# Loading and transposing the second batch's q and k in another split and order, in a fused attention and gate kernel

## The chip, the core and the metric

The kernel runs on one core of a Trainium2 chip. The metric is the device time of one execution in microseconds; the time shown for a kernel is the median of several executions.

## What is computed

Attention over 4 batches, 8 heads, 768 positions and a head size of 64, in which a query sees the 128 positions that end with its own and the first 4 positions of the sequence (sinks), and behind it a highway layer on the 3072 rows of 512:

```
scores = q @ k.T / 8, kept where 0 <= query - key < 128 or key < 4
a = softmax(scores);  x = a @ v            # heads side by side: 3072 x 512
H = relu(x @ w_h);  T = sigmoid(x @ w_t + b_t)
out = T * H + (1 - T) * x                  # float32
```

All inputs are float32 in the chip's main memory. Matrix products run in float16 with float32 sums.

## The kernel before

**Steps.** The 3072 rows are cut into 24 tiles n of 128 rows, 6 for each batch. The program is written as one loop over n, in which the stages of several tiles are interleaved, and the order in which the calls stand is the order on each engine: a last pass chains the instructions of every engine in that order, so that no engine overtakes itself. In step n stand the scores of tile n, the values of tile n-1 and the gate of tile n-2.

- `opening(n, n-1, n-2)` puts the mask matmuls (L308, L318), the 32 score matmuls of tile n (L333, `product`), the bias of the gate (L371) and the sink part (L379) on TensorE. In steps 5 and 6 the scores stand alone (`scores(n)`), then `hidden` of an older tile, and then the rest of the opening. The scores of tile c of a batch take the q of tiles c and c+1 (two column blocks) and the k of tile c.
- `expo(n)`: ScalarE's exponential E (L421), 128x2048, in the last tile of a batch 128x1024. Its starts mark the steps in the text: E(n).
- `values(n-1)`: TensorE, E times v (L432, L435), needs the v tile in float16, made by `cast_v` (L150), on VectorE up to tile 5 and on GpSimd (POOL) from tile 6 on.
- `norm(n-1)`: VectorE, reciprocal (L443) and product X (L445). Then `x_transpose` (L461) on TensorE and `x_copy` (L466) on ScalarE.
- `gate(n-2)` (L471) with w_t, `tanh` (L479), `hidden` (L492) with w_h into the one buffer `ps_h`, `diff` (L505, VectorE, reads `ps_h`), later `gated` (L510), `finish` (L516, mostly POOL) and the store. Since w_h is loaded late, `hidden(0)` and `diff(0)` stand in step 4, `hidden(1)`, `diff(1)` and `hidden(2)`, `diff(2)` in step 5, `hidden(3)` in step 6.

**Loads.** q and k are cast to float16 on the way by DMAs that POOL issues; POOL's queue also carries w_t, w_h and the bias. A batch's positions are split in `segments`: three thirds of 256 for batches 0 and 1, two halves of 384 for batches 2 and 3; they are called (batch, part) here, as in q(1,0). `load_part` (L117) loads one of the four row groups g of a part: 32 partitions, 2 head groups, 64 KB as float16 in a third. Four of them make a part of q or k. v comes by `load_v` (L140) from SyncE, 256 KB a tile; the loads of v(2) to v(7) are tied to the score matmuls of an earlier step.

Before the loop POOL issues k(0,0), k(0,1), w_t, the bias, q(0,2), k(0,2) and w_h; then, in step 2, the sink values of batch 0, q(1,0) and k(1,0), and from there a written list of counts for each step:

```
issues = [(b, i, g, which) for b in range(1, B) ...][2 * G:]
for n, count in zip(range(2, 17), [4] * 4 + [3] * 7 + [2] + [3] * 3):
    loads[n] = [issues.pop(0) for _ in range(count)]
```

so that q(1,1), k(1,1), q(1,2), k(1,2) stand in steps 2 to 5, and batch 2 begins in step 6. From step 6 on POOL's turn in a step is `cast_v`, loads, `finish` of older tiles (`completed`).

**Transposes.** `transpose_qk` (L133) transposes 32x32 blocks of a loaded part on VectorE, from `nat` to `tr`: 128x512 float32 words for a whole third, both head groups at once. `units` says in which step: q(1,0) in step 4, k(1,0) in step 5, ahead of `diff(1)` and `norm(4)`, q(1,1) in 6, k(1,1) and q(1,2) in 7, k(1,2) in 8. Of batch 0, q(0,2) is transposed in step 2 and k(0,2) in step 3, both behind the step's `norm`.

Of the kernel before, what the change touches and what calls it, by code (L numbers as in the profile page):

```python
# [37 lines left out]
def kernel(  # L38
# [14 lines left out]
    pe, act, dve, pool, sp = nc.tensor, nc.scalar, nc.vector, nc.gpsimd, nc.sync  # L53

    B, H, S, D = q.shape
# [10 lines left out]
    G = 4  # L66
# [43 lines left out]
    def v_of(n):  # L110
        return vt[n % 8]

    def load_part(b, i, g, which, into=None, engine=pool):

        t0, nt = segments[b][i]
        into = nat[b][i][:, which] if into is None else into
        engine.dma_start(  # L117
            out=into[32 * g:32 * g + 32].rearrange("p hg m d -> p hg (m d)"),
            in_=(q, k)[which][b, :, t0:t0 + nt, :].rearrange(
                "(hg g) (r m) d -> g r hg (m d)", g=G, m=nt // 32)[g])  # L120

    def load_rows(b, i, which):
        for g in range(G):
            load_part(b, i, g, which)

    def transpose_qk(b, i, which, hgs=slice(0, HG)):

# [9 lines left out]
    def load_v(n, after=None):  # L137
        b, t = divmod(n, NC)
        V32[n] = work.tile([P, H, D], FP32, tag="V32", name="V32", bufs=8)
        ins = sp.dma_start(out=V32[n],  # L140
                           in_=v[b, :, t * P:(t + 1) * P, :].transpose([1, 0, 2]))
        if after is not None:
            tc.add_manual_dep(
                ins.ins, after.ins.name,
                mybir.DependencyInfo(
                    mybir.DependencyClass.Sync, mybir.DependencyReason.DATA),
                reason="behind the loads needed first")

    def cast_v(n, engine):
        engine.tensor_copy(out=v_of(n)[:, :, 0:D], in_=V32[n])  # L150
# [32 lines left out]
    def load_sinks(b, gs=range(G)):  # L183
        for g in gs:
# [7 lines left out]
    load_rows(0, 0, 1)  # L192
# [7 lines left out]
    load_v(1)  # L200
    load_sinks(0, range(2, G))
    make_identity(nc, ident)
    load_rows(0, 1, 1)
    pool.dma_start(out=wt, in_=moe_w_t.rearrange("(kc p) of -> p kc of", p=P))
    pool.dma_start(out=brow[0:P:32, :], in_=moe_b_t.unsqueeze(0).to_broadcast([G, DM]))
    load_rows(0, 2, 0)
    load_rows(0, 2, 1)
    pool.dma_start(out=wh, in_=moe_w_h.rearrange("(kc p) of -> p kc of", p=P))

    dve.memset(ebias, _EXP_BIAS)  # L210
# [337 lines left out]
    for b in range(1, B):  # L548
# [8 lines left out]
    issues = [(b, i, g, which) for b in range(1, B) for i in range(len(segments[b]))  # L557
              for which in range(2) for g in range(G)][2 * G:]
    loads = {}
    for n, count in zip(range(2, 17), [4] * 4 + [3] * 7 + [2] + [3] * 3):  # L560
        loads[n] = [issues.pop(0) for _ in range(count)]
    assert not issues
    v_at = {1: (2,), 2: (3,), 3: (4,), 4: (5,), 5: (6, 7), 6: (8, 9)}
    for n in range(7, N):
        v_at[n] = (n + 3,)
    completed = {6: (0, 1), 7: (2,)}
    completed.update({n: (n - 5,) for n in range(8, 21)})
    completed.update({21: (16, 17), 22: (18, 19)})


# [16 lines left out]
    transpose_qk(0, 1, 0)  # L587
    cast_v(0, dve)
    sink_keys(0, dve)

    idle(18)
    last = N - 1
    for n in range(last):

        nb, n1 = n - 2, n - 1
        joined = n < 5 or n >= 7
        before = (n1 if 0 <= n1 < N else None, nb if nb >= 0 else None)
        if n < N:
            after = opening(n, *before) if joined else scores(n)
            expo(n)  # L600
            if n in (4, 5):
                gate_value(n - 4)
            if n > NC and n % NC == NC - 1:
# [12 lines left out]
        if 0 <= n1 < N:  # L616
            values(n1)
        if n >= 6:
            cast_v(n, pool)
        if NC <= n < N and n % NC == 0:  # L620
            sink_keys(n // NC)
        if n == 2:
            sink_values(0)
            load_rows(1, 0, 0)
            load_rows(1, 0, 1)
        for b, i, g, which in loads.get(n, ()):
            load_part(b, i, g, which)
        if n > NC and n % NC == 1:
            sink_values(n // NC)

        done = list(completed.get(n, ()))
        if n == 6:
            while done:
                complete(done.pop(0))
        turn = list(units.get(n, ()))
        if n == 5:
            transpose_qk(*turn.pop(0))
        if 5 <= n <= 6:
            diff(1 if n == 5 else 3)
# [135 lines left out]
```

## Time and profile before

| | |
|---|---|
| median of 3 runs | 108.6 us (107.96 to 109.45) |
| profiled execution | 108.8 us, its span 106.8 us, 2.0 us around it |
| TensorE, VectorE, ScalarE, POOL busy | 95.6, 85.6, 80.5, 83.6 us |
| granted TensorE clock, mean | 0.996 |
| DMA | 20.81 MB, 195 GB/s mean |

The profile is of one execution. Times in it are counted from the start of the span. An engine's row in the timeline tells its start, its duration, the engine, the source line and what is written from what; in brackets stand the idle time before it and what ended that. A DMA's row under the issuing engine is the time of issuing it, and the list of DMA issues tells how long after its issue the data had landed.

### The profile page before, as it was taken

How to read it: one execution, taken by the hardware profiler on the slowest of the kernel's cores; microseconds unless marked ns; L12 is line 12 of the kernel's file. 1: busy time of each engine (PE TensorE's matmuls, PEld its weight loads, DVE VectorE, ACT ScalarE, POOL GpSimd, SP SyncE). 2: the span in 40 equal slices, each digit the busy share in tenths (PEclk: the TensorE clock that was granted, in tenths of full speed). 3: DMA queues.
4: the chain of work that ended last, by engine and by line, in shares of the span. 5: the costliest groups of instructions: out<-in, count | busy, mean ns of one | idle time of the engine just before them, and what ended most of it. 6: DMA issues, size and time to landing. Idle time of an engine off the chain costs nothing. (4 is left out here: it accounts for less than half of the span.)

```text
span 106.8 us, 4671 instructions
## 1 busy us (share of the span) xinstructions
PE 95.6 (90%) x1960; PEld 53.0 (50%) x1960; DVE 85.6 (80%) x187; ACT 80.5 (75%) x105; POOL 83.6 (78%) x139
## 2 busy tenths in 40 slices
PE   5997785988779999999999999999999999999930
PEld 2333452555325545655565556555655565465610
DVE  6998647555497879889988987899889979998960
ACT  3386687779648598798868997898689978986750
POOL 6899549918797999999999999999577829778000
PEclk9999999999999999999999999999999999999998
DMA  3999999999999988789999998999995763252523
GB/s 77 225 260 225 200 215 196 151 179 232 212 213 237 176 151 240 133 213 250 223 208 269 250 249 190 235 235 211 221 296 126 201 181 114 104 198 84 214 84 114
DMA packets 36388, 20.81 MB, mean 195 GB/s; under 512 B 27020, under 2 KB 32912, under 8 KB 36368
## 3 DMA queue, kind: packets, MB, share of 16 engines
q1 hardware_dynamic: 29216, 13.31, 47.1%
q0 software_dynamic: 6848, 6.82, 40.7%
q10 hardware_dynamic: 304, 0.39, 1.2%
q8 instruction: 15, 0.25, 1.0%
q14 instruction: 5, 0.04, 0.1%
HBM read 21.05 MB, written 6.29 MB: 256 GB/s over the span
## 5 line engine op out<-in xcount | busy, mean ns | idle before, releaser
L421 ACT ACTIVATE E<-ps_s,ebias 128x2048 f16<-128x2048 f32 (+1 forms) x24 | 43.8, 1824 | 10.8 <-PE ps_s L333 10.8
L133 DVE STREAM_TRANSPOSE tr<-nat 128x384 f32<-128x384 f32 (+1 forms) x28 | 26.1, 962 | 3.7 <-DMA nat<-in_q_dram 2.1
L492 PE MATMUL ps_h<-wh,XT 128*128 128x512 f16 (+1 forms) x96 | 27.2, 375 | 1.8 <-DVE DD L505 1.8
L117 POOL DMA_DIRECT2D nat<-in_k_dram x40 | 21.8, 549 | 7.0 <-DMA wh<-in_moe_w_h_dram 2.6
L516 POOL TENSOR_TENSOR O<-DD,X 128x512 f32<-128x512 f16 x19 | 22.0, 1160 | 6.6 <-DVE DD L510 4.0
L471 PE MATMUL ps_z<-wt,XT 128*128 128x512 f16 (+1 forms) x96 | 24.3, 374 | 0.0
L505 DVE SCALAR_TENSOR_TENSOR DD<-ps_h,X 128x512 f16<-128x512 f32 (+1 forms) x24 | 16.1, 673 | 3.6 <-PE ps_h L492 3.6
L117 POOL DMA_DIRECT2D nat<-in_q_dram x32 | 17.8, 562 | 0.2
L466 ACT COPY XT<-ps_av 128x512 f16<-128x512 f16 x23 | 13.5, 586 | 4.4 <-PE ps_av L461 2.2
L445 DVE TENSOR_TENSOR X<-ps_av,rec 128x512 f16<-128x512 f32 x23 | 15.9, 691 | 0.8
L479 ACT ACTIVATE TH<-ps_z 128x512 f16<-128x512 f32 (+1 forms) x24 | 14.0, 582 | 3.2 <-PE ps_z L471 3.2
L333 PE MATMUL ps_s<-tr 32*64 32x192 f16 (+3 forms) x768 | 13.3, 240 | 1.2 <-DVE tr L133 1.2
L435 PE MATMUL ps_av<-v,E 128*128 128x65 f16 x184 | 13.4, 193 | 0.2
L492 PEld LDWEIGHTS <-XT 128*128 128x128 f16 x100 | 8.8, 98 | 8.4 <-issue 2.3
L432 PEld LDWEIGHTS <-E 128*128 128x128 f16 x160 | 10.3, 97 | 4.1 <-issue 3.2
L432 PE MATMUL ps_av<-v,E 128*128 128x65 f16 x152 | 12.4, 194 | 0.0
L435 PEld LDWEIGHTS <-E 128*128 128x128 f16 x192 | 11.8, 97 | 0.7 <-issue 0.6
L150 POOL CAST v<-V 128x512 f16<-128x512 f32 x18 | 11.9, 663 | 0.0
L333 PEld LDWEIGHTS <-tr 32*64 32x64 f16 x768 | 10.3, 104 | 1.9 <-issue 1.0
L471 PEld LDWEIGHTS <-XT 128*128 128x128 f16 x100 | 8.2, 98 | 5.9 <-issue 0.5
L510 DVE TENSOR_TENSOR DD<-DD,TH 128x512 f16<-128x512 f16 (+1 forms) x23 | 10.1, 444 | 0.8
L461 PEld LDWEIGHTS <-X 128*128 128x128 f16 x96 | 5.8, 97 | 9.5 <-DVE X L445 8.9
(90 smaller groups left out, 115.0 us busy)
## 6 DMA issues: line engine op xcount, KB each, us to landing
V<-in_v_dram SPq DMA_DIRECT2D x24, 256.0 KB, 4.7
out_dram<-O SPq DMA_DIRECT2D x23, 256.0 KB, 3.7
nat<-in_k_dram POOLq DMA_DIRECT2D x24, 64.0 KB, 4.6
nat<-in_q_dram POOLq DMA_DIRECT2D x16, 96.0 KB, 4.7
nat<-in_k_dram POOLq DMA_DIRECT2D x16, 96.0 KB, 4.6
nat<-in_q_dram POOLq DMA_DIRECT2D x16, 64.0 KB, 5.6
first<-in_q_dram SPq DMA_DIRECT2D x6, 128.0 KB, 3.7
wt<-in_moe_w_t_dram POOLq DMA_DIRECT2D x1, 512.0 KB, 7.3
```

Of the source, the lines that this page charges most:

```text
L117: engine.dma_start(out=into[32 * g:32 * g + 32].rearrange("p hg m d -> p hg (m d)"), in_=(q, k)[which][b, :, t0:t0 + nt, :].rearrange("(hg ...
L133: dve.transpose(out=dst, in_=src)
L333: return pe.matmul(ps_s[ks, g, hg, q0:q1], lhsT=tr[b][rows, 1, hg, k0:k0 + K2, e], rhs=tr[b][rows, 0, hg, c * P + q0:c * P + q1, e], start ...
L421: act.activation(out=E[n][:, :, :, 0:nq * P], in_=ps_s[:, :, :, 0:nq * P], func=AF.Exp, bias=ebias, scale=SCALE)
L432: pe.matmul(slot, lhsT=E[n - 1][:, g, hg, P:2 * P], rhs=v_of(n - 1)[:, h, :], start=first, stop=False, skip_group_check=True)
L435: pe.matmul(slot, lhsT=E[n][:, g, hg, 0:P], rhs=v_of(n)[:, h, :], start=first, stop=True, skip_group_check=True)
L445: dve.tensor_tensor(out=X[n], in0=av[:, :, :, 0:D], in1=rec.unsqueeze(3).to_broadcast([P, HG, G, D]), op=ALU.mult)
L471: pe.matmul(into, lhsT=XT[n][:, kc * P:(kc + 1) * P], rhs=wt[:, kc, cols], start=False, stop=(kc == KC - 1), skip_group_check=True)
L479: act.activation(out=TH[n][:, cols], in_=ps_z if z is None else z, func=AF.Tanh, scale=0.5)
L492: pe.matmul(into, lhsT=XT[n][:, kc * P:(kc + 1) * P], rhs=wh[:, kc, cols], start=(kc == 0), stop=(kc == KC - 1), skip_group_check=True)
L505: dve.scalar_tensor_tensor(out=DD[n][:, cols], in0=ps_h[:, cols] if h is None else h, scalar=0.0, in1=flat(X[n], cols), op0=ALU.max, op1=A ...
L516: eng.tensor_tensor(out=O[n][:, cols], in0=DD[n][:, cols], in1=flat(X[n], cols), op=ALU.add)
```

## The change

- A half-head load, `load_heads(b, i, hg, which)`, is added: one of the two head groups of a part over all 128 partitions, 128 KB as float16, two for a part. q(1,1), k(1,1) and q(1,2) are loaded with it (steps 3, 4 and 5, two a step), tied to the score matmuls of the step before; k(1,2) stays in four row groups, in step 5.
- The first row group of q(1,0) is issued ahead of w_h. The other seven parts of q(1,0) and k(1,0), and ahead of them the sink values of batch 0, move from step 2 to before the loop.
- The counts of the loads of batches 2 and 3 for each step change: 4 in step 6, then 3, 2, 3, 3, 3, 3, 1, 3, 3, 3, 1.
- In step 6 `cast_v(6)` moves behind the step's loads.
- k(0,2) is transposed in two halves by head group, one in step 2 behind `cast_v(2)`, one in step 3 behind `norm(2)`.
- `diff(0)` goes ahead of the transpose of q(1,0); `diff(1)` and `norm(4)` go ahead of the transpose of k(1,0).
- `completed`: tile 2 is finished in step 8 together with tile 3, and not in step 7.

The order on TensorE and on ScalarE stays the same instruction by instruction. On SyncE one v load and one store change places.

```diff
+    def behind(ins, after):
+        if after is not None:
+            tc.add_manual_dep(...)
-    def load_part(b, i, g, which, into=None, engine=pool):
+    def load_part(b, i, g, which, into=None, engine=pool, after=None):
 ...
+    def load_heads(b, i, hg, which, after=None):
+        t0, nt = segments[b][i]
+        ins = pool.dma_start(
+            out=nat[b][i][:, which, hg].rearrange("p m d -> p (m d)"),
+            in_=(q, k)[which][b, :, t0:t0 + nt, :].rearrange(
+                "(hg g) (r m) d -> hg g r (m d)", g=G, m=nt // 32)[hg])
+        behind(ins, after)
 ...
+    load_part(1, 0, 0, 0)
     pool.dma_start(out=wh, in_=moe_w_h.rearrange("(kc p) of -> p kc of", p=P))
 ...
+    loads = {3: [], 4: [], 5: []}
+    for n, i, which in ((3, 1, 0), (4, 1, 1), (5, 2, 0)):
+        loads[n] += [(load_heads, 1, i, hg, which) for hg in range(HG)]
+    loads[5] += [(load_part, 1, 2, g, 1) for g in range(G)]
+    issues = [(load_part, b, i, g, which) for b in range(2, B) ...]
+    for n, count in zip(range(6, 18), (4, 3, 2, 3, 3, 3, 3, 1, 3, 3, 3, 1)):
         loads[n] = [issues.pop(0) for _ in range(count)]
-    completed = {6: (0, 1), 7: (2,)}
-    completed.update({n: (n - 5,) for n in range(8, 21)})
+    completed = {6: (0, 1), 8: (2, 3)}
+    completed.update({n: (n - 5,) for n in range(9, 21)})
 ...
     sink_keys(0, dve)
+    sink_values(0)
+    for g in range(1, G):
+        load_part(1, 0, g, 0)
+    for g in range(G):
+        load_part(1, 0, g, 1)
 ...
-        if n >= 6:
+        if n > 6:
             cast_v(n, pool)
-        if n == 2:
-            sink_values(0)
-            load_rows(1, 0, 0)
-            load_rows(1, 0, 1)
-        for b, i, g, which in loads.get(n, ()):
-            load_part(b, i, g, which)
+        for load, *args in loads.get(n, ()):
+            load(*args, after=before_n if n <= 5 else None)
+        before_n = after
+        if n == 6:
+            cast_v(n, pool)
 ...
-        if n == 5:
-            transpose_qk(*turn.pop(0))
         if n == 3:
-            transpose_qk(0, 2, 1)
+            transpose_qk(0, 2, 1, slice(1, 2))
 ...
+        if n == 2:
+            transpose_qk(0, 2, 1, slice(0, 1))
-        for unit in turn:
+        for unit in turn if n != 4 else ():
             transpose_qk(*unit)
 ...
             hidden(0)
             diff(0)
+            transpose_qk(*turn.pop())
             cast_v(n, dve)
```

More of the change, by code (lines that the diff above doesn't have):

```diff
@@ L111, in v_of @@
         return vt[n % 8]
-    def load_part(b, i, g, which, into=None, engine=pool):
+    def behind(ins, after):
+        if after is not None:
+            tc.add_manual_dep(
+                ins.ins, after.ins.name,
+                mybir.DependencyInfo(
+                    mybir.DependencyClass.Sync, mybir.DependencyReason.DATA),
+                reason="behind the loads needed first")
+    def load_part(b, i, g, which, into=None, engine=pool, after=None):
         t0, nt = segments[b][i]
         into = nat[b][i][:, which] if into is None else into
-        engine.dma_start(
+        ins = engine.dma_start(
             out=into[32 * g:32 * g + 32].rearrange("p hg m d -> p hg (m d)"),
@@ L120, in load_part @@
                 "(hg g) (r m) d -> g r hg (m d)", g=G, m=nt // 32)[g])
-    def load_rows(b, i, which):
-        for g in range(G):
-            load_part(b, i, g, which)
+        behind(ins, after)
[5 more added lines that the diff above has]
+                "(hg g) (r m) d -> hg g r (m d)", g=G, m=nt // 32)[hg])
+        behind(ins, after)
     def transpose_qk(b, i, which, hgs=slice(0, HG)):
@@ L141, in load_v @@
                            in_=v[b, :, t * P:(t + 1) * P, :].transpose([1, 0, 2]))
[L142 to L147, printed above, removed]
+        behind(ins, after)
     def cast_v(n, engine):
@@ L191 @@
               allow_small_or_imprecise_dtypes=True)
-    load_rows(0, 0, 1)
+    for g in range(G):
+        load_part(0, 0, g, 1)
     for g in range(G):
@@ L202 @@
     make_identity(nc, ident)
-    load_rows(0, 1, 1)
+    for g in range(G):
+        load_part(0, 1, g, 1)
     pool.dma_start(out=wt, in_=moe_w_t.rearrange("(kc p) of -> p kc of", p=P))
     pool.dma_start(out=brow[0:P:32, :], in_=moe_b_t.unsqueeze(0).to_broadcast([G, DM]))
-    load_rows(0, 2, 0)
-    load_rows(0, 2, 1)
+    for which in range(2):
+        for g in range(G):
+            load_part(0, 2, g, which)
+    load_part(1, 0, 0, 0)
     pool.dma_start(out=wh, in_=moe_w_h.rearrange("(kc p) of -> p kc of", p=P))
@@ L556 @@
                 units.setdefault(n, []).append((b, i, which, slice(hg, hg + 1)))
[L557 to L560, printed above, removed]
+    loads = {3: [], 4: [], 5: []}
+    for n, i, which in ((3, 1, 0), (4, 1, 1), (5, 2, 0)):
+        loads[n] += [(load_heads, 1, i, hg, which) for hg in range(HG)]
+    loads[5] += [(load_part, 1, 2, g, 1) for g in range(G)]
+    issues = [(load_part, b, i, g, which) for b in range(2, B) for i in range(len(segments[b]))
+              for which in range(2) for g in range(G)]
+    for n, count in zip(range(6, 18), (4, 3, 2, 3, 3, 3, 3, 1, 3, 3, 3, 1)):
         loads[n] = [issues.pop(0) for _ in range(count)]
@@ L589 @@
     sink_keys(0, dve)
+    sink_values(0)
+    for g in range(1, G):
+        load_part(1, 0, g, 0)
+    for g in range(G):
+        load_part(1, 0, g, 1)
     idle(18)
```

1 line of the change is left out of this document (removed).

## Prediction

> **What bounds the kernel now.** I read the page first, then ScalarE's timeline, whose exponentials mark the steps, then VectorE, TensorE, POOL and the DMA issues around the slow steps. From the page the span and the mean busy share of the DMA engines in 40 slices of 2.67 us; from ScalarE's timeline E(4) to E(7), E(10), E(13) and E(19):
>
> ```profile
> span 106.8 us, 4671 instructions
> DMA  3999999999999988789999998999995763252523
> 22.77 1.97 ACT L421 ACTIVATE E<-ps_s,ebias 128x2048 f16<-128x2048 f32 x1 [0.61 <-PE ps_s L333]
> 26.97 1.11 ACT L421 ACTIVATE E<-ps_s,ebias 128x1024 f16<-128x1024 f32 x1
> 33.11 1.97 ACT L421 ACTIVATE E<-ps_s,ebias 128x2048 f16<-128x2048 f32 x1 [0.21 <-PE ps_s L333]
> 37.65 1.97 ACT L421 ACTIVATE E<-ps_s,ebias 128x2048 f16<-128x2048 f32 x1 [0.59 <-PE ps_s L333]
> 48.50 1.97 ACT L421 ACTIVATE E<-ps_s,ebias 128x2048 f16<-128x2048 f32 x1 [0.49 <-PE ps_s L333]
> 58.78 1.97 ACT L421 ACTIVATE E<-ps_s,ebias 128x2048 f16<-128x2048 f32 x1 [0.47 <-PE ps_s L333]
> 79.91 1.97 ACT L421 ACTIVATE E<-ps_s,ebias 128x2048 f16<-128x2048 f32 x1 [0.48 <-PE ps_s L333]
> ```
>
> From E(7) on the pace is even: E(7), E(13) and E(19) lie 21.13 us apart. So what E(7) gains should reach the end. Up to E(7) it is uneven: E(4) to E(7) takes 14.88 us, the same steps a batch later, E(10) to E(13), 10.28. The surplus is 4.6 us, the largest single step E(5) to E(6) with 6.14. The DMA engines are at 90% or more in every slice up to 37 us. VectorE and then TensorE in that stretch:
>
> ```profile
> 25.81 1.11 DVE L133 STREAM_TRANSPOSE tr<-nat 128x512 f32<-128x512 f32 x1 [1.32 <-DMA nat<-in_q_dram]
> 26.77 0.67 DVE L505 SCALAR_TENSOR_TENSOR DD<-ps_h,X 128x512 f16<-128x512 f32 x1
> 27.52 0.43 DVE L150 CAST v<-V 128x512 f16<-128x512 f32 x1
> 29.35 1.11 DVE L133 STREAM_TRANSPOSE tr<-nat 128x512 f32<-128x512 f32 x1 [1.40 <-DMA nat<-in_k_dram]
> 30.31 0.67 DVE L505 SCALAR_TENSOR_TENSOR DD<-ps_h,X 128x512 f16<-128x512 f32 x1
> 31.12 0.69 DVE L445 TENSOR_TENSOR X<-ps_av,rec 128x512 f16<-128x512 f32 x1
> 32.09 0.69 DVE L505 SCALAR_TENSOR_TENSOR DD<-ps_h,X 128x512 f16<-128x512 f32 x1
> ...
> 24.34 1.03 PE L492 MATMUL ps_h<-wh,XT 128*128 128x512 f16 x4
> 27.49 1.02 PE L492 MATMUL ps_h<-wh,XT 128*128 128x512 f16 x4 [1.08 <-DVE DD L505]
> 28.79 0.20 PE L432 MATMUL ps_av<-v,E 128*128 128x65 f16 x1
> 31.03 1.02 PE L492 MATMUL ps_h<-wh,XT 128*128 128x512 f16 x4 [0.72 <-DVE DD L505]
> 32.35 0.66 PE L333 MATMUL ps_s<-tr 32*64 32x192 f16 x32
> 32.95 1.04 PE L492 MATMUL ps_h<-wh,XT 128*128 128x512 f16 x4
> ```
>
> The two transposes (q(1,0), then k(1,0)) wait 1.32 and 1.40 us for their loads, and behind them in order stand `diff(0)`, and `diff(1)` with `norm(4)`. `ps_h` is one buffer, so `hidden(1)` waits 1.08 us for `diff(0)` and `hidden(2)` 0.72 us for `diff(1)`; the scores of tile 6 come after these in TensorE's order. Behind VectorE's waits stand POOL and its queue:
>
> ```profile
> 15.78 0.78 POOL L208 DMA_DIRECT2D wh<-in_moe_w_h_dram x1
> 24.33 0.53 POOL L117 DMA_DIRECT2D nat<-in_k_dram  x1 [2.64 <-DMA wh<-in_moe_w_h_dram]
> 31.54 0.72 POOL L117 DMA_DIRECT2D nat<-in_q_dram  x1
> 35.06 0.62 POOL L150 CAST v<-V 128x512 f16<-128x512 f32 x1
> ...
> wh<-in_moe_w_h_dram POOLq DMA_DIRECT2D x1, 512.0 KB, 8.3
> nat<-in_q_dram POOLq DMA_DIRECT2D x1, 64.0 KB, 5.2
> ```
>
> A load on POOL waits for the landing of the eighth load before it: the last part of k(1,0) stood 2.64 us for w_h. The q row (5.2 us to landing) is the last part of q(1,2), issued at 31.54.
>
> **The change part by part.** (1) *Order on VectorE in steps 4 and 5.* The two waits go from in front of `diff(0)`, `diff(1)` and `norm(4)` to behind them. What then comes late first is w_h and v(4). One q part (64 packets) now goes ahead of w_h. Its price comes from the list of queues between 18.5 and 22.5 us, in which w_h's packets fill the engines, and from SyncE's rows:
>
> ```profile
> q0 software_dynamic: 529, 0.53, 99.2%
> q1 hardware_dynamic: 17, 0.00, 0.5%
> ...
> 19.23 0.37 SPq L140 DMA_DIRECT2D V<-in_v_dram  x1
> 19.65 2.91 SPq L186 DMA_DIRECT2D vs<-in_v_dram  x4
> V<-in_v_dram SPq DMA_DIRECT2D x1, 256.0 KB, 8.3
> ```
>
> 529 packets in 4.0 us make 64 packets 0.48 us. w_h landed at 15.78 + 8.3 = 24.1, now at 24.55, so `hidden(0)` starts at 24.55 instead of 24.34, ends at 25.6, and `diff(0)` at 26.25. Then the q transpose to 27.35, and `hidden(1)`, 1.08 us earlier than 27.49, at about 26.4.
>
> v(4) decides next: its load, issued at 19.23, landed 8.3 us later, at 27.5, when VectorE cast it (row 27.52). It got next to nothing while w_h's packets ran (17 packets of its queue against 529), so w_h's delay passes on to it. The bounds are 0 and 0.48 us; I take 0.3, nearer the delay's own row than nothing. `cast_v(4)` then runs from 27.8 to 28.25, `values(4)` starts at 28.3 instead of 28.79. From there TensorE was busy 28.79 to 30.31 (31.03 less its wait of 0.72), 1.52 us; so `hidden(2)` starts at 29.8, for `diff(1)` is done at 28.25 + 0.7. From `hidden(2)` to E(6) it took 33.11 - 31.03 = 2.08: E(6) at 31.9, **1.2 us earlier**. The k transpose must be done at 29.8 + 1.3 (scores at 32.35): `norm(4)` from 29.0 to 29.9, transpose to 30.95; it fits by 0.15 us, given k(1,0) at 29.9. That load, now waiting for the q part ahead of w_h instead of for w_h, is issued near 22 instead of 24.33.
>
> Then `cast_v(5)` to 31.3 and `diff(2)` to 32.0. `hidden(3)` (row 32.95) stood right behind the scores and would start at 31.75; it waits to 32.0: 0.25 is lost. From it to E(7) it took 37.65 - 32.95 = 4.7: E(7) at 36.7, **0.95 earlier**.
>
> (2) *k(0,2) in halves.* Step 2's `norm`, step 3's old transpose, and the landing of the last part of k(0,2), issued at 15.26:
>
> ```profile
> 20.09 0.21 DVE L443 RECIPROCAL rec<-ps_av 128x8 f32<-128x8 f32 x1 [1.26 <-PE ps_av L435]
> 20.94 1.10 DVE L133 STREAM_TRANSPOSE tr<-nat 128x512 f32<-128x512 f32 x1
> nat<-in_k_dram POOLq DMA_DIRECT2D x1, 64.0 KB, 4.5
> ```
>
> A half, 0.55 us by size, was to fit into VectorE's 1.26 us before 20.09. But k lands at 15.26 + 4.5 = 19.8, so it ends at 20.35 and holds `norm(2)` by 0.25; the second half ends at 20.35 + 0.9 + 0.55 = 21.8 instead of 22.0. Bounds -0.2 and +0.25; I take 0.
>
> (3) *Half-head loads.* Twelve issues of 0.53 us become six, each between 0.53 (64 KB) and w_h's 0.78 (512 KB), say 0.6: POOL is free 2.8 us more. It waited for landings there, so I count nothing. They matter by what waits for them: VectorE needs q(1,1) near 34 us and k(1,1) near 37.5, and POOL must issue four loads of q(2,0), the last behind the landing of the second half of q(1,2), before `cast_v(6)`, which moves behind them. That half is issued at about 28 (after w_h's landing at 24.55, six issues of 0.6). If it lands as the last q part did, after 5.2 us and 64 packets more (0.48), it is there at 33.7; if the full DMA engines bring it no earlier than before, at 31.54 + 5.2 = 36.7. I take the middle, 35.2: `cast_v(6)` is done 0.53 + 0.62 later, at 36.35. `values(6)` is wanted when E(7) starts, 36.7. So it is hidden, by 0.35 us.
>
> (4) *`gated(2)` from step 7 to 8*:
>
> ```profile
> 41.62 0.40 DVE L510 TENSOR_TENSOR DD<-DD,TH 128x512 f16<-128x512 f16 x1
> ```
>
> VectorE goes into `norm(7)` behind it; 0 to 0.4 us less there, given back in part in step 8. I take 0.15.
>
> (5) The counts from step 6 on, `finish(2)` and the exchanged store and v load on SyncE cost nothing: POOL issues as much as before and arrives earlier; if its cover went, it would be the case of `cast_v(6)`.
>
> Sum: 0.95 + 0.15 = 1.1. The profiled execution took 108.8 (span 106.8 and 2.0 around it) and would take 107.7; it lies 0.2 above the median of the runs, 108.6, which gives **107.5 us**.
>
> SyncE's four sink loads of 4 KB, taken from four heads each, cost 2.91 us to issue, 0.73 each, against 0.37 for a v load of 256 KB. The Trainium skill, page "DMA: Bandwidth & Descriptors", section "Why a DMA increments its semaphore by 16 and not by 1", has a copy run on the largest number of engines up to 16 that divides the slowest dimensions of both sides; it knows exceptions for GpSimd's copies. By it a half-head load, four heads outermost on the source side, runs on 4 engines, which is the slower rival below; by the rows of the row-group loads it runs on 16, and the sum stands.
>
> **The rivals.** *Slower: half-head loads land late on few engines.* A load has 128 packets of 2 KB read: 8 on each of 16 engines, 32 on each of 4. At 16 x 4.0 / 529 = 0.12 us a packet that is 2.9 us more. The second half of q(1,2) then lands between 35.2 + 2.9 = 38.1 and 36.7 + 2.9 = 39.6, `cast_v(6)` is done 1.15 later, and against E(7)'s old 37.65 `values(6)` is 1.6 to 3.1 late: 110.2 to 111.7, middle **110.9**. It decides from a landing after 36.5 on. For it speaks the price of the sink loads' issue; against it that w_h, four packets for every one of these, was done in 8.3 us, and that the loads are issued 3.5 us earlier.
>
> *No change: the engines are full.* All slices to 37 us are at 9, so reordering brings no byte sooner in all. With the half landing at 36.7, `cast_v(6)` ends at 37.85 and the gain of E(7) is used up: **108.6**. Against it: POOL's waits for landings, 2.64 us in one place, show that the queue ran dry of issued loads now and then.
>
> *More: the surplus goes.* If v(4) lands at 27.5 as before, E(6) gains 1.5; and if the loads, issued earlier, stop holding any engine up to E(7), half of the 4.6 us goes with 0.4 from step 7: 2.7, **105.9**. For it speaks that every wait of the stretch ends at a load or at something queued behind one; against it that TensorE is nearly filled from 28.3 on.
>
> **How the numbers follow.** Forecast 0.43, more 0.28, no change 0.17, slower 0.12. Faster by over 2% (below 106.4), about what a measurement of this kernel can tell from no change, takes most of the case "more" and a small part of the forecast's spread: 0.30. Slower by over 2% (above 110.8) is half of the slow case and little else: 0.08. Within 2%: 0.62. The range reaches from 105.6, a little under the case "more", to 110.4, into the slow case's lower end; about 0.1 lies outside on each side.
>
> **What would show it.** Right: VectorE's L133 rows of q(1,0) and k(1,0) behind L505 and L445; no TensorE wait for L505 before the second `hidden` of step 5; E(6) near 31.9, E(7) near 36.7; E(7) to E(13) still 21.1. Wrong: v(4) landing after 28.5; `cast_v(6)` ending after E(7) starts, with TensorE waiting for POOL; half-head loads with over 8 us to landing; the end of E(4) to E(7) no nearer than 14.5 us.

## The result, and the profile after

The changed kernel takes 111.85 us (median of 6 runs, 110.81 to 115.25), the kernel before 108.28 beside it: a ratio of 1.030, 95% interval [1.021, 1.038]. It is slower, and 107.5 was forecast. The ratio, here and below, compares only the faster executions of each kernel and leaves out those in a slower state, so it is not the quotient of the two medians. The profiled execution took 111.51 us.

First the page of the profile after: the span, the granted clock and the DMA engines' busy share in 40 slices (2.74 us each), the queue of POOL's copies (packets, MB, share), and two rows of the list of DMA issues (count, KB each, us from issue to landing), those of the half-head loads.

```profile
span 109.5 us, 4664 instructions
PEclk9999999999999958999999999999999999999999
DMA  3999999999699998996999998999997735341523
q0 software_dynamic: 9056, 6.83, 41.4%
nat<-in_q_dram POOLq DMA_DIRECT2D x4, 128.0 KB, 9.1
nat<-in_k_dram POOLq DMA_DIRECT2D x2, 128.0 KB, 8.1
```

In the slice from 27.4 to 30.1 us, in which the half-head loads are under way, the DMA engines are busy to 6 tenths and move 74 GB/s; in before they are at 9 in every slice around that time. So full engines alone do not explain the 8 to 9 us of these loads.

Then E(4), E(6), E(7), E(8) and E(13) in ScalarE's timeline:

```profile
22.88 1.97 ACT L437 ACTIVATE E<-ps_s,ebias 128x2048 f16<-128x2048 f32 x1 [0.27 <-PE ps_s L349]
31.65 1.97 ACT L437 ACTIVATE E<-ps_s,ebias 128x2048 f16<-128x2048 f32 x1 [0.28 <-PE ps_s L349]
36.45 1.97 ACT L437 ACTIVATE E<-ps_s,ebias 128x2048 f16<-128x2048 f32 x1 [0.59 <-PE ps_s L349]
43.62 1.97 ACT L437 ACTIVATE E<-ps_s,ebias 128x2048 f16<-128x2048 f32 x1 [0.47 <-PE ps_s L349]
61.28 1.97 ACT L437 ACTIVATE E<-ps_s,ebias 128x2048 f16<-128x2048 f32 x1 [0.47 <-PE ps_s L349]
```

E(6) and E(7) come 1.46 and 1.20 us earlier than before (33.11, 37.65). Then E(8) comes 7.17 us after E(7), where it took 3.24 before (40.89): it stands 2.73 late. E(13) is 2.50 late and the last exponential, E(23), 2.70, so in this execution all that was lost was lost in this one step. POOL and TensorE in it:

```profile
38.05 0.53 POOL L125 DMA_DIRECT2D nat<-in_q_dram  x1 [0.69 <-DMA nat<-in_q_dram]
38.58 0.62 POOL L160 CAST v<-V 128x512 f16<-128x512 f32 x1
...
39.25 0.60 PE L451 MATMUL ps_av<-v,E 128*128 128x65 f16 x8 [2.66 <-POOL v L160]
39.66 1.90 PE L487 MATMUL ps_z<-wt,XT 128*128 128x512 f16 x4
```

`cast_v(6)` stands behind the four loads of q(2,0); the last of these waits for the landing of the second half of q(1,2), at 37.77, and is issued at 38.05. The cast ends at 39.20 and `values(6)` (L451) has waited 2.66 us. After the wait the clock is down: the gate's four matmuls take 1.90 us, and 1.02 elsewhere. The stage by windows, of after and, in the second line, of before (length, busy time and count of each engine, clock, DMA share, GB/s):

```profile
36.45:43.62 7.17, 4.51 (x68) 2.31 (x64) 3.48 (x5) 3.15 (x4) 6.05 (x10) 0.76 1.10 240
...
37.65:40.89 3.24, 3.24 (x68) 1.75 (x64) 2.59 (x4) 2.93 (x3) 3.23 (x5) 1.00 0.75 169
```

The same 68 rows of TensorE lasted 4.51 us at a mean clock of 0.76, against 3.24 at 1.00.

### The profile page after: what moved, and what is told of

Its sections match the earlier page's. It is cut to its first block, busy times and chain, and to the rows that moved or that the text cites. A ratio compares the mean times of both kernels' runs of the same rounds, so it can differ in the third digit from the quotient of the medians.

```text
span 109.5 us, 4664 instructions
## 1 busy us (share of the span) xinstructions
PE 95.9 (88%) x1960; PEld 53.4 (49%) x1960; DVE 86.8 (79%) x188; ACT 81.0 (74%) x105; POOL 81.1 (74%) x133
## 3 DMA queue, kind: packets, MB, share of 16 engines
q0 software_dynamic: 9056, 6.83, 41.4%
## 5 line engine op out<-in xcount | busy, mean ns | idle before, releaser
L148 DVE STREAM_TRANSPOSE tr<-nat 128x384 f32<-128x384 f32 (+2 forms) x29 | 26.3, 935 | 1.4 <-DMA nat<-in_k_dram 1.1
L487 PE MATMUL ps_z<-wt,XT 128*128 128x512 f16 (+1 forms) x96 | 25.2, 384 | 0.4 <-issue 0.4
L125 POOL DMA_DIRECT2D nat<-in_k_dram x36 | 19.8, 557 | 5.9 <-DMA wt<-in_moe_w_t_dram 2.8
L451 PE MATMUL ps_av<-v,E 128*128 128x65 f16 x184 | 13.8, 195 | 3.1 <-POOL v L160 2.7
L125 POOL DMA_DIRECT2D nat<-in_q_dram x24 | 13.1, 555 | 3.0 <-DMA nat<-in_k_dram 1.8
L451 PEld LDWEIGHTS <-E 128*128 128x128 f16 x192 | 11.9, 99 | 3.4 <-issue 3.2
L459 DVE RECIPROCAL rec<-ps_av 128x8 f32<-128x8 f32 x23 | 4.7, 202 | 9.7 <-PE ps_av L451 9.4
```

Source lines behind the costliest of these rows:

```text
L125: ins = engine.dma_start(out=into[32 * g:32 * g + 32].rearrange("p hg m d -> p hg (m d)"), in_=(q, k)[which][b, :, t0:t0 + nt, :].rearrang ...
L148: dve.transpose(out=dst, in_=src)
L451: pe.matmul(slot, lhsT=E[n][:, g, hg, 0:P], rhs=v_of(n)[:, h, :], start=first, stop=True, skip_group_check=True)
L487: pe.matmul(into, lhsT=XT[n][:, kc * P:(kc + 1) * P], rhs=wt[:, kc, cols], start=False, stop=(kc == KC - 1), skip_group_check=True)
```

## The experiments

Each group ran on one chip beside the kernel before. The theories: *loads* (half-head loads are slow and hold `cast_v(6)`), *order* (`cast_v(6)` only stands in the wrong place), *clock*, and later *meeting* (a VectorE product held by a POOL sum) and *queue* (POOL's work from step 6 to 9 is full, and takes back what TensorE gains).

### The cast, the loads, the clock

`cast_first`, the changed kernel with the cast back in its place:

```diff
-        if n > 6:
+        if n >= 6:
             cast_v(n, pool)
 ...
-        if n == 6:
-            cast_v(n, pool)
```

> The changed kernel with cast_v(6) back ahead of step 6's loads, nothing else. Theory of the order (the loss is POOL's: cast_v(6) stands behind four loads of q(2,0), the last of which waits for the landing of the second half of q(1,2)): cast_v(6) now waits only for v(6), landed at 35.1, and is done before E(7) at 36.5; E(8) near 39.8, the time near 107.6. Theory of the loads (the half-head loads themselves cost, because they hold a few DMA engines and the v loads behind them): v(7) still lands near 39.4, so cast_v(7) takes the place of cast_v(6) and the time stays at 108.5 to 110.

`row_groups`, the changed kernel with row-group loads in the same steps:

```diff
-        loads[n] += [(load_heads, 1, i, hg, which) for hg in range(HG)]
+        loads[n] += [(load_part, 1, i, g, which) for g in range(G)]
```

> The changed kernel with q(1,1), k(1,1) and q(1,2) in four row groups each, as k(1,2) is, at the same places and behind the same waits; cast_v(6) stays behind step 6's loads. Theory of the loads: the last load of q(1,2) lands by 35.5 instead of 37.8, cast_v(6) is done by 36.7, and the time is 107.5 to 108.2. Theory of the order alone: the wait in front of cast_v(6) is the same in kind, the DMA engines being full, and the time stays above 110.

`rows_cast`, both edits:

> Both edits: row groups for the six half-head loads' parts, and cast_v(6) ahead of step 6's loads. Both theories: the gain of E(7), 1.2 us, is kept; 107.0 to 107.6. If it is not below the kernel before, something else of the change costs (w_h later, k(0,2) in halves, tile 2 finished in step 8).

`warm`, the changed kernel with matmuls on zeros in TensorE's idle time, so that the clock stays up:

```diff
+        if n == 7:
+            idle(12)
         if 0 <= n1 < N:
             values(n1)
```

> The changed kernel with 12 matmuls of zeros into the free buffer of hidden, about 2.6 us, in TensorE's order ahead of values(6), where it sat idle for 2.7 us. Theory of the clock: the granted clock of 0.53 between 38.5 and 41.0 comes of that idle time and costs 0.9 us in gate(5) and hidden(5); with the filling the clock stays at 1.0 and the time falls by 0.7 to 1.1 to about 110.6. Rival: the clock is not the cost, and the time stays at 111.5 or above.

Measured: 111.41 (ratio 1.022 [1.013, 1.031]), 110.41 (1.017 [1.008, 1.026]), 110.54 (four runs, 108.30 to 110.77, no ratio) and 111.39 (1.025 [1.016, 1.034]), before 108.69. No edit came clearly back to the kernel before, so the change holds more than one cost. `cast_first` and `warm` lie in neither of their ranges; `row_groups` misses the theory of the loads and lies where the order alone was expected, above 110. Its rows, POOL, then TensorE:

```profile
38.45 0.62 POOL L160 CAST v<-V 128x512 f16<-128x512 f32 x1
39.13 0.42 PE L451 MATMUL ps_av<-v,E 128*128 128x65 f16 x8 [1.75 <-POOL v L160]
39.38 1.03 PE L487 MATMUL ps_z<-wt,XT 128*128 128x512 f16 x4
```

With row groups the cast ends at 39.07, hardly before the 39.20 of after. The last row group of q(1,2) landed 5.1 us after its issue, but it was issued at 32.55 only, for the first of the part had waited until 30.97 (a load waits for the landing of the eighth before it, and row groups are twice as many); so it was there at 37.62, and the second half in after at 37.77. So behind these loads the cast is late with either shape. From E(7) to E(8) it takes 5.06 us in `row_groups`, 7.17 in after, 3.26 in `cast_first`, and 3.26 in `tile2_rows` below, which has both edits: as before, 3.24.

What the shape does is seen at v. The loads of v(6) and v(7) landed at 31.10 and 33.05 us in before, at 32.36 and 33.68 in `row_groups`, but at 35.14 and 39.41 in after and at 36.66 and 39.94 in `cast_first`. In `cast_first` two waits are left. VectorE, POOL and TensorE in steps 6 to 8:

```profile
46.76 2.17 DVE L526 TENSOR_TENSOR DD<-DD,TH 128x512 f16<-128x512 f16 x1
36.72 0.61 POOL L160 CAST v<-V 128x512 f16<-128x512 f32 x1 [2.81 <-DMA V<-in_v_dram]
47.46 1.17 POOL L532 TENSOR_TENSOR O<-DD,X 128x512 f32<-128x512 f16 x1
42.74 0.19 PE L451 MATMUL ps_av<-v,E 128*128 128x65 f16 x1 [1.66 <-POOL v L160]
49.82 0.34 PE L477 MATMUL ps_av<-ident,X 128*128 128x128 f16 x3 [1.37 <-DVE X L461]
```

E(8) stood at 40.80, as before (40.89), though the lead of E(7) was gone by then: E(7) stood at 37.54. `cast_v(6)` had waited 2.81 us for v(6), the rest of POOL's work came later, and TensorE waits 1.66 us for `cast_v(7)`: E(9) is 1.56 late. Then `gated(3)`, 0.43 us elsewhere, lasts 2.17, until 0.3 us after POOL's sum of tile 2, which the change has put there; `norm(8)` is behind it and TensorE waits 1.37 us. E(10) is 2.88 late. The product began 0.70 us before the sum's row; why it was not done by then is not shown.

In `warm` the second half of q(1,2) landed at 38.84, 1.07 us later than in after, and the cast ended at 40.72, so its time says nothing of the clock; its stage does. With the idle time filled the gate takes 1.02 us, and from the cast's end to E(8) it takes 43.94 - 40.72 = 3.22 us, in after 43.62 - 39.20 = 4.42. The slower clock cost about 1.2 us, by one execution of each.

```profile
41.03 1.02 PE L487 MATMUL ps_z<-wt,XT 128*128 128x512 f16 x4
43.94 1.97 ACT L437 ACTIVATE E<-ps_s,ebias 128x2048 f16<-128x2048 f32 x1 [0.60 <-PE ps_s L349]
```

### The parts alone

`only_tile2`, the kernel before with one edit, and `tile2_rows` and `tile2_heads`, `rows_cast` and `cast_first` with this edit undone:

```diff
-    completed = {6: (0, 1), 7: (2,)}
-    completed.update({n: (n - 5,) for n in range(8, 21)})
+    completed = {6: (0, 1), 8: (2, 3)}
+    completed.update({n: (n - 5,) for n in range(9, 21)})
```

> The kernel before with tile 2 finished in step 8 instead of step 7, and nothing else. Theory of the meeting: GpSimd adds tile 2 just as VectorE wants gate_value(3) or gated(3) in step 8, one of them is held to the end of that sum, 0.5 to 1.5 us: 109.2 to 110.2. Rival: the two miss one another at this pace, or the delay is hidden: 108.4 to 108.9, and then the meeting hurts only together with the later loads.

> rows_cast with tile 2 finished in step 7 again, as before the change. Theory of the meeting: in rows_cast the product gated(3) on VectorE lasted 2.17 us, from 45.26 to the end of GpSimd's sum of tile 2 (45.97 to 47.14), where the same product has 0.43 us when GpSimd does not add at that time; norm(8) and with it E(10) came 1.4 us late by that. With tile 2 back in step 7 the product is 0.43 again and the time falls by 1.4 to 2.0 us, from 110.5 to 108.5 to 109.1. Rival, that the later place of the tile costs nothing and the rest is in the transfers: 110.2 to 110.6.

> cast_first (half-head loads kept, cast_v(6) ahead of the loads) with tile 2 finished in step 7 again. Theory of the meeting: cast_first had the same 2.17 us product, E(10) 1.3 us late by it, and a wait of 1.66 us for cast_v(7) that this edit leaves: 111.4 - 1.4 = 110.0, range 109.5 to 110.4. Beside tile2_rows it gives the price of the half-head loads alone: 1 to 1.5 us if the wait for cast_v(7) stays, none if it goes. Rival, that the later place of the tile costs nothing: 111.2 to 111.6.

Measured: `only_tile2` 109.51 (1.014 [1.008, 1.021]), `tile2_rows` 109.65 (1.015 [1.009, 1.021]), `tile2_heads` 110.68 (1.021 [1.012, 1.030]), before 108.93. The move of tile 2 alone costs 1.4% by the runs. In its trace E(10) is 0.92 us late against the trace of before, and 0.4 from E(16) to the end, so the size is uncertain. Undoing the move brought the medians down by 0.9 and 0.7 us, on another chip and less than expected (the four runs of `rows_cast` scatter by more than that), and the ratio of `tile2_heads` is that of `cast_first`: what was won there went into another wait. In `only_tile2` it is `gate_value(3)`, 0.28 us elsewhere, that POOL's sum holds:

```profile
44.96 1.55 DVE L486 TENSOR_SCALAR TH<-TH 128x512 f16<-128x512 f16 x1
45.18 1.17 POOL L516 TENSOR_TENSOR O<-DD,X 128x512 f32<-128x512 f16 x1
```

The Trainium skill, page "GPSIMD Engine Reference", section "1. Specifications", has GpSimd share its SBUF interfaces with VectorE, in contention with VectorE instructions that have two SBUF inputs or run in a two-port mode. These rows agree with it for a product of two SBUF tensors. A scaling of one was held too; no row shows its mode. The rows with an input in PSUM kept their durations beside the sums, `norm`'s product 0.69 us and `diff` 0.66 to 0.70, in all the runs here.

`tile2_rows` shows where the rest is, POOL, TensorE and E(8), E(9):

```profile
37.76 2.28 POOL L532 TENSOR_TENSOR O<-DD,X 128x512 f32<-128x512 f16 x2
39.99 0.81 POOL L160 CAST v<-V 128x512 f16<-128x512 f32 x1
...
40.86 0.21 PE L451 MATMUL ps_av<-v,E 128*128 128x65 f16 x1 [1.73 <-POOL v L160]
41.65 1.90 PE L487 MATMUL ps_z<-wt,XT 128*128 128x512 f16 x4
...
38.85 1.97 ACT L437 ACTIVATE E<-ps_s,ebias 128x2048 f16<-128x2048 f32 x1 [0.32 <-PE ps_s L349]
46.26 1.97 ACT L437 ACTIVATE E<-ps_s,ebias 128x2048 f16<-128x2048 f32 x1 [0.30 <-PE ps_s L349]
```

Here every load of q(1,1) to q(1,2) goes by row groups and the cast is in its old place. E(8) is 2 us ahead of before, so the loss of step 6 is gone, and then the whole lead and more goes in the next step: `cast_v(7)` stands on POOL behind four loads and two sums, TensorE waits 1.73 us for it, and loses its clock on top.

`only_order`, the kernel before with VectorE's new order alone:

```diff
-        if n == 5:
-            transpose_qk(*turn.pop(0))
 ...
-        for unit in turn:
+        for unit in turn if n != 4 else ():
             transpose_qk(*unit)
 ...
             diff(0)
+            transpose_qk(*turn.pop())
             cast_v(n, dve)
```

> The kernel before with VectorE's new order in steps 4 and 5 alone: diff(0) ahead of the transpose of q, diff(1) and norm(4) ahead of that of k; all loads, casts and finishes as before. Forecast's theory: E(6) and E(7) come 1.0 to 1.4 us earlier, as they did after the change, and nothing else loses it: 107.1 to 107.6. Rival, that the pace of steps 7 to 9 is set by the landing of v and by GpSimd's order, and takes the gain back: 108.3 to 108.8.

Measured: 108.58, 1.005 [1.000, 1.009]. The rival holds. E(6), E(8) and E(10), and POOL, whose last row is that of before:

```profile
31.52 1.97 ACT L421 ACTIVATE E<-ps_s,ebias 128x2048 f16<-128x2048 f32 x1 [0.45 <-PE ps_s L333]
39.61 1.97 ACT L421 ACTIVATE E<-ps_s,ebias 128x2048 f16<-128x2048 f32 x1 [0.33 <-PE ps_s L333]
48.15 1.97 ACT L421 ACTIVATE E<-ps_s,ebias 128x2048 f16<-128x2048 f32 x1 [0.49 <-PE ps_s L333]
...
43.04 1.14 POOL L516 TENSOR_TENSOR O<-DD,X 128x512 f32<-128x512 f16 x1
44.14 0.67 POOL L150 CAST v<-V 128x512 f16<-128x512 f32 x1
...
44.55 0.60 POOL L150 CAST v<-V 128x512 f16<-128x512 f32 x1
```

The order does what was forecast: E(6) and E(8) are 1.59 and 1.28 us early. E(10) is 0.35 early. POOL works without a pause from 34.6 us on, and `cast_v(8)` ends at 44.81, nearly where it ended before (45.16).

### Half-head loads alone, and why they are slow

`only_heads`, the kernel before with the six half-head loads in place of the twelve; `pair_heads`, the same with each of them cut in two by heads, so twelve loads of 64 KB again:

```diff
+        for p in range(2):
             pool.dma_start(
-                out=nat[b][i][:, which, hg]...,
-                in_=(q, k)[which][...].rearrange("(hg g) (r m) d -> hg g r (m d)", ...)[hg])
+                out=nat[b][i][64 * p:64 * p + 64, which, hg]...,
+                in_=(q, k)[which][...].rearrange(...)[hg, 2 * p:2 * p + 2])
```

> The kernel before with q(1,1), k(1,1) and q(1,2) loaded by halves of the heads, six loads in place of twelve, in the same steps 2 to 4, and nothing else. In it cast_v(6) stands ahead of the loads of step 6, so slow transfers can only hold the transposes of steps 6 and 7, and v. Theory of the slow loads: the six loads take 7 to 10 us to landing as after the change, v(6) lands near 35 and v(7) near 38, and the pace of steps 6 and 7 loses 0.5 to 1.5 us: 109.4 to 110.4. Rival, that their landing hurts only through the order of GpSimd's work: 108.5 to 109.1.

> only_heads with each half-head load cut in two by pairs of heads: twelve loads of 64 KB as in the kernel before, the same bytes and the same number of issues, but each covers 64 partitions in two pieces of 32 rows, where a row group of before has its 32 rows as the outermost dimension. Theory of the few engines: a load goes to as many transfer engines as its outermost dimension has entries (2 here, 4 in only_heads, all 16 for a row group), each load brings some 460 four-byte packets (32 for each of 14 idle engines, and 16), the loads take 7 us and more to landing and the time is 109.5 to 112. Rival, that the price is in the 128 KB of one load or in the rows being read head by head: as before, 108.0 to 108.8, with some 16 four-byte packets a load.

Measured: `only_heads` 109.94 (1.019 [1.015, 1.024], before 108.29) and `pair_heads` 112.16 (1.040 [1.033, 1.048], before 107.98). The half-head loads alone cost 1.9%; halved in size and doubled in number they cost twice as much. The issues from 24.2 to 30 us of `only_order`, which loads by row groups, and of `pair_heads`, and then POOL's queue over the whole of before, of `only_heads` and of `pair_heads`:

```profile
V<-in_v_dram SPq DMA_DIRECT2D x3, 256.0 KB, 4.7
nat<-in_k_dram POOLq DMA_DIRECT2D x5, 64.0 KB, 4.7
nat<-in_q_dram POOLq DMA_DIRECT2D x4, 64.0 KB, 4.5
...
V<-in_v_dram SPq DMA_DIRECT2D x3, 256.0 KB, 8.2
nat<-in_k_dram POOLq DMA_DIRECT2D x5, 64.0 KB, 7.1
nat<-in_q_dram POOLq DMA_DIRECT2D x4, 64.0 KB, 6.1
...
q0 software_dynamic: 6848, 6.82, 40.7%
q0 software_dynamic: 9056, 6.83, 41.4%
q0 software_dynamic: 12224, 6.85, 43.3%
```

The same number of loads of the same size land 1.6 to 2.4 us later, and v, on another queue, 3.5 us later. The packets say why. All that is added are packets of 4 bytes, 1212, 3420 and 6588 in the three traces; those with data stay 5636. If each idle engine of a load gets 32 of them, and each load 16 more, `pair_heads` has 12 x 14 x 32 = 5376 more than before, which is 12224 - 6848 to the packet, and `only_heads` 6 x (12 x 32 + 16) - 12 x 16 = 2208 = 9056 - 6848. So the half-head loads ran on 4 of 16 engines and the pairs on 2; the packets do not name their engine, but both counts fit exactly. That is the rule of the Trainium skill, page "DMA: Bandwidth & Descriptors", section "Why a DMA increments its semaphore by 16 and not by 1", which the prediction gave to its slower rival: the number of engines is the largest up to 16 that divides the slowest dimension of both sides, with 4 heads or 2 on the source here, 32 rows in a row group.

### POOL's queue

`order_casts`, `cure_rows` and `cure_heads` are `only_order`, `tile2_rows` and `tile2_heads` with the casts of v(7) to v(9) one step forward, ahead of the sums:

```diff
-        if n >= 6:
+        if n >= 6 and n not in (7, 8, 9):
             cast_v(n, pool)
 ...
+        if n in (6, 7, 8):
+            cast_v(n + 1, pool)
         done = list(completed.get(n, ()))
```

> only_order with the casts of v(7), v(8) and v(9) on GpSimd moved one step forward, from the head of steps 7 to 9 to just ahead of the finishing sums of steps 6 to 8. Theory of GpSimd's order: in only_order E(8) stood 1.28 us earlier than before and E(10) only 0.35, since cast_v(8) came behind sink_values and the sum of tile 2 (43.04 to 44.14) and ended at 44.81, at the same time as before; with the cast ahead of that sum E(10) is 0.7 to 0.9 us earlier: 107.6 to 108.0. Rival, that the gain goes in a later stage anyway: 108.4 to 108.8.

> tile2_rows (row-group loads, cast_v(6) ahead of the loads, tile 2 finished in step 7) with the same three casts moved forward. Theory of GpSimd's order: tile2_rows had E(8) at 38.85, 2 us earlier than the kernel before, then TensorE waited 1.73 us for cast_v(7), which stood behind four loads and the sums of tiles 0 and 1, and its clock fell behind that wait (the four gate matmuls took 1.90 us where they take 1.02); E(9) came 7.42 us after E(8). With the cast ahead of the sums both go, E(9) comes 4 us after E(8), and the time falls by 1.5 to 2.5 us: 107.2 to 108.2. Rival, that slow transfers set that stage: 109.2 to 109.7.

> tile2_heads, which keeps the half-head loads, with the same three casts moved forward. Theory of GpSimd's order: its 7.06 us from E(8) to E(9) fall to 4, and the time falls by 1.5 to 2.5 us: 108.2 to 109.2. Theory of the slow loads: v(7) and v(8) land late, the moved casts then hold the loads and sums behind them on GpSimd, and the time stays within 110.0 to 111.0. Beside cure_rows it gives the price of the half-head loads where nothing else of the change stands in the way.

Measured: 109.15 (1.011 [1.005, 1.017]), 109.33 (1.007 [1.003, 1.012]) and 111.32 (1.026 [1.017, 1.034]), before 108.29. All three miss the theory of POOL's order; `cure_rows` lies in the range of its rival. The casts came early, but the sums moved into the way of VectorE's products; `cure_heads`:

```profile
40.27 2.27 POOL L532 TENSOR_TENSOR O<-DD,X 128x512 f32<-128x512 f16 x2
...
41.03 1.81 DVE L526 TENSOR_TENSOR DD<-DD,TH 128x512 f16<-128x512 f16 x1
```

Then sums were taken out of the full stage. `later_finish`, `later_rows` and `later_before` are `only_order`, `tile2_rows` and the kernel before with one tile a step:

```diff
-    completed = {6: (0, 1), 7: (2,)}
-    completed.update({n: (n - 5,) for n in range(8, 21)})
+    completed = {n: (n - 7,) for n in range(7, 17)}
+    completed.update({17: (10, 11), 18: (12,), 19: (13,), 20: (14, 15)})
```

> only_order with the finishing sums spread: one tile a step from step 7 on (tile n - 7 in step n up to step 16, two in steps 17 and 20), none in step 6. Theory of GpSimd's queue: in only_order GpSimd has no pause from 34.6 to 50 us and cast_v(8) ends at 44.81 behind three sums (3.4 us); with two of them gone it ends near 42.5, the 0.94 us that E(8) to E(10) lose against the kernel before stay won: 107.3 to 107.8. Rival, that the gain goes to the next wait on the list (landing of k, TensorE's own work) or that the late finishes cost at the end: 108.4 to 108.9.

> tile2_rows (the change with row-group loads, cast_v(6) ahead of the loads and tile 2 not in step 8) with the same spread of the finishing sums. Theory of GpSimd's queue: TensorE's wait of 1.73 us for cast_v(7) and the slower clock behind it go, E(9) comes 4 us after E(8) instead of 7.42: 109.65 less 2 to 3 us, 106.8 to 107.8. Rival: 108.8 to 109.7, if another wait takes its place.

> The kernel before with the same spread of the finishing sums and VectorE's old order. Theory of GpSimd's queue: in the kernel before GpSimd's casts end just in time (cast_v(8) at 45.16, TensorE waits 0.2 us), so little is to be had, 107.9 to 108.4, and later_finish is faster than this by 0.5 to 1 us, the price of VectorE's order. Rival: as much is won here as in later_finish, and VectorE's order is worth nothing.

Measured: 109.18 (1.008 [1.004, 1.012]), 110.14 (1.010 [1.002, 1.019]) and 109.72 (1.015 [1.009, 1.021]), before 107.98. All are slower than before and than expected; E(10), E(13) and E(19) of `later_finish`:

```profile
47.36 1.97 ACT L421 ACTIVATE E<-ps_s,ebias 128x2048 f16<-128x2048 f32 x1 [0.42 <-PE ps_s L333]
57.65 1.97 ACT L421 ACTIVATE E<-ps_s,ebias 128x2048 f16<-128x2048 f32 x1 [0.47 <-PE ps_s L333]
79.67 1.97 ACT L421 ACTIVATE E<-ps_s,ebias 128x2048 f16<-128x2048 f32 x1 [0.52 <-PE ps_s L333]
```

With POOL relieved a gain passes through: E(10) and E(13) are 1.14 and 1.13 us early. But `later_before`, with VectorE's old order, has E(13) 0.62 early, so VectorE's order is worth 0.51 of it; between the medians of the two lie 0.54 us. From E(13) to E(19) it takes 22.02 instead of 21.13, and from E(19) to E(23) 14.70 instead of 14.08: steps 17 and 20, which make up two tiles, give the gain back.

`one_later` and `one_later_rows` take one sum out of the stage and leave VectorE's products where they are (`finish` of tiles 1 to 14 one step later, behind that step's `gated`; step 20 makes up the one, where POOL has a pause):

```diff
-        finish(m, eng=dve if m >= N - 3 else pool)
+        if not 1 <= m <= 14:
+            finish(m, eng=dve if m >= N - 3 else pool)
 ...
+        if n == 20:
+            finish(14)
         for m in done[-1:] if n < last - 1 else ():
-            complete(m)
+            done_m = complete(m)
+        if 7 <= n < 20:
+            finish(n - 6, after=done_m)
```

> only_order with each GpSimd sum of tiles 1 to 14 one step later (tile n - 6 in step n, each behind that step's own product on VectorE, the lag closed in step 20, where GpSimd waits 1.9 us in the kernel before); VectorE's products stay where they are. Theory of GpSimd's queue: one sum (1.15 us) less stands ahead of cast_v(7) and cast_v(8), the 0.94 us that only_order loses between E(8) and E(10) shrink to 0.2, E(10) comes near 47.4, and, other than in later_finish, no step has two products to make up at the end: 107.6 to 108.0, faster than both kernels if by little. Rival: another wait takes it, 108.4 to 108.8.

> tile2_rows with the same sums one step later. Theory of GpSimd's queue: cast_v(7) ends 1.1 us earlier than 40.80, TensorE waits 0.5 instead of 1.73 us for it, its clock is kept, and E(9) comes near 44 instead of 46.26: 109.65 less 1 to 2 us, 107.7 to 108.7. Rival: 109.2 to 109.8.

Measured: `one_later` 107.89, 0.996 [0.993, 0.999], and `one_later_rows` 108.17, 1.001 [0.997, 1.004], before 108.30. `one_later` is the only version whose interval lies below the kernel before, by 0.4%; within 2% this counts as the same time. E(13) and E(19), VectorE, and POOL with `cast_v(8)`:

```profile
57.80 1.97 ACT L421 ACTIVATE E<-ps_s,ebias 128x2048 f16<-128x2048 f32 x1 [0.47 <-PE ps_s L333]
78.43 1.97 ACT L421 ACTIVATE E<-ps_s,ebias 128x2048 f16<-128x2048 f32 x1 [0.47 <-PE ps_s L333]
...
44.09 0.28 DVE L486 TENSOR_SCALAR TH<-TH 128x512 f16<-128x512 f16 x1
44.41 0.43 DVE L510 TENSOR_TENSOR DD<-DD,TH 128x512 f16<-128x512 f16 x1
...
42.44 0.61 POOL L150 CAST v<-V 128x512 f16<-128x512 f32 x1
```

`cast_v(8)` ends at 43.05 instead of 44.81, no product is held in that step, and E(19) keeps its lead: 78.43 against 79.91. The two traces are 1.5 us apart and the medians 0.4: the profiled execution of `one_later`, 107.30, was its fastest, and that of before, 108.8, lies above its median. That one sum less, with the same loads as in `tile2_rows`, brings 1.015 to 1.001, and E(9) from 1.33 us late to 0.89 early, shows POOL's queue as what held that kernel back.

## Why the prediction was wrong

- **(1), VectorE's order: right, its size in part by luck.** E(6) at 31.9 was forecast and 31.65 measured, E(7) at 36.7 and 36.45. The same program up to there put E(7) at 37.54 in `cast_first` and at 37.31 in `warm`, so one trace could not be hit to 0.25 us but by chance. v(4) was not delayed by w_h at all: it landed at 25.7, not 27.8, 6.5 us after its issue. `hidden(0)` was 0.3 later than forecast (24.83).
- **(2), k(0,2) in halves: right within its bounds at E(4),** which came 0.11 late. The half began at 20.14 and took 0.65 us, not 0.55, and `norm(2)` came 0.54 late, not 0.25.
- **(3), the half-head loads: the step that failed.** The mis-sized term is the landing of the second half of q(1,2): 35.2 was taken, 36.7 was the upper bound, and it measured 37.77. Issued at 28.10, as forecast (28), it took 9.67 us. The sum took the time to landing from a load of another shape, 5.2 us, added its bytes, and took the middle between that and "no earlier than before". The runs showed in its place that the loads ran on few engines (`pair_heads`), and that the term would not have come out with row groups either, which landed at 37.62 (`row_groups`). So `cast_v(6)`, put behind these loads, ended at 39.20 and not at 36.35, and `values(6)` was late by 2.66 us instead of early by 0.35. Only with the cast back in its place was this wait gone. Two of the signs named ahead for a wrong forecast came: TensorE waiting for POOL after E(7), and half-head loads with over 8 us to landing.
- **The slower rival had the mechanism, and its number partly by luck.** Its 110.9 us is near the 111.5 of the profiled execution, but the half landed at 37.77, ahead of its 38.1 to 39.6; what made up for that is the slower clock, which it did not have. Its chance of 0.12 was too low, on the ground that w_h, a bigger load, had taken 8.3 us.
- **The rival "the engines are full" rested on a reading that was not quite so:** the first slice is at 3, not 9, and in after a slice with the half-head loads under way was at 6.
- **What no term held: the clock.** A wait was priced at its length; behind this one the clock cost 1.2 us more (`warm`).
- **(4), tile 2 to step 8: wrong in sign by its own run.** 0.15 us gain was taken; alone it costs 1.4%, 0.4 us of it seen in the trace. The step looked at VectorE, from which a product goes away, and not at what runs beside that product on POOL in its new place. In after itself little of this is paid, since step 8 comes late there anyway: `gate_value(3)` took 0.69 and `gated(3)` 0.42.
- **"What E(7) gains should reach the end": wrong.** It was read from the even pace from E(7) on. POOL's casts keep that pace in steps 7 to 9, so E could come early and wait (`only_order`). POOL's relief was counted as nothing at (3) and (5), and just there was the bound. With POOL relieved, about 0.5 us of VectorE's order reached the end (`later_finish` against `later_before`).
- **Open.** Costs of 1.9% (`only_heads`) and 1.4% (`only_tile2`) add up to the 3.0% measured only roughly; they share waits. The cast's new place was not run alone on the kernel before. Between `tile2_rows` and the kernel before other small edits differ as well (the counts of loads, the q part ahead of w_h, the loads moved ahead of the loop and their ties, k(0,2) in halves); each of these alone was not run.

## What to carry to other kernels

Cost a changed load by its outermost dimension before its bytes: merging issues into fewer, bigger loads can take it from 16 engines to 4, and then it slows its neighbours on other queues as well. Do not put work that the next step needs behind loads that wait for other loads: here it came late with either shape. Before a gain in one engine's order is counted to the end, follow the next engines in their own written order, and see whether the value that the early work needs next is made early too. When work is moved to another step, look at what runs beside it there, not only at its own engine.

## What the runs showed of the hardware

- A 128x512 float16 product on VectorE took 0.43 us alone and up to 2.17 beside a POOL sum (`cast_first`), a scaling of the same size 0.28 and up to 1.61 (`warm`); held so, the product ended 0.3 us after the sum's end and the scaling 0.16. POOL's cast held a product to 0.71.
- TensorE's clock fell behind idle times of 2.66, 1.73 and 1.46 us (after, `tile2_rows`, `tile2_heads`), and not behind 2.00, 1.75 and 1.66 (`pair_heads`, `row_groups`, `cast_first`). The length alone does not decide.
- In some runs TensorE stood still inside the gate's four matmuls of step 4, for nothing that the profile names: 0.41 us in after, 1.27 in `cast_first`, 1.06 in `row_groups`. In each it went on 1.4 to 1.5 us after a 16 KB packet of the instruction queue had arrived, and in before, where that packet came 0.7 to 1.7 us earlier, the second of the four began 0.40 us behind the first, where without a stop it is 0.22. Late instruction fetch behind full DMA engines would explain it; no run tested that.
